# Key sums beside the second product transposed and added in one VectorE operation; their reciprocals stored and spread from GpSimd's queue

## The chip, the cores and the metric

The kernel runs on one core of a Trainium2 chip. Its time is the device time of one execution in microseconds (us). The profile calls the engines PE (TensorE, matmuls), PEld (TensorE's weight loads), DVE (VectorE), ACT (ScalarE), POOL (GpSimd) and SP (SyncE, which here only issues DMAs). Each of them works through its own instructions in the order in which the program gives them.

## The reference

Attention with normalised queries and keys, and after it two matrix products with a squared ReLU between them. All tensors are float32; q, k and v have 8 batches of 12 heads, 448 rows and 64 columns, and the products have 3584 rows, 768 columns and 2048 hidden columns.

```python
q_n, k_n = rmsnorm(q, g_q), rmsnorm(k, g_k)
scores = scale * np.matmul(q_n, k_n.transpose(0, 1, 3, 2))
scores = scores - np.max(scores, axis=-1, keepdims=True)
attn = np.exp(scores)
attn = attn / (np.sum(attn, axis=-1, keepdims=True) + 1e-09)
attn_out = np.matmul(attn, v)
...
x = attn_out.transpose(0, 2, 1, 3).reshape(B * S, H * D)
h = x @ w_in
r = np.maximum(h, 0.0)
return (r * r) @ w_out
```

## The kernel before

**Stages.** The batches are taken two at a time, in four spans. A span has two batches of six head pairs, so 12 pairs, which I call units, numbered through (`i`). The attention of the first span runs alone. After it each span has a first product (line 1040) and a second product (line 1087). Both are written as seven block products in place of eight (a Strassen form), so that VectorE and GpSimd have sums of blocks to make beside them. In the first three spans the second product and the attention of the next span are woven together: one is a generator with a step for each matmul, the other a generator with five steps for each unit, and the loop at the end of the kernel takes from both in turn. In the first span this stage also holds `combine` (lines 1001 to 1005), the block sums for its second product, on VectorE. Only in these three stages does the changed code run, 12 units in each, 36 in all.

**A unit of attention there** (function `attention`, line 945). Keys lie on partitions. `scores(i, c)` multiplies a chunk of 128 keys (`c` from 0 to 2; chunk 3 has the last 64) with all queries, into one of two PSUM buffers, and ScalarE writes the exponential (line 761) into one of five places: four tiles `pr` and the half `qkT[:, 1]`, taken in turn, `places[(3 * i + c) % 5]`; chunk 3 has a tile of its own, `half`. `values(i)` (line 837) multiplies the exponentials with v, one unit later. For the denominators VectorE adds the four chunks into `acc` (`add_up`, lines 782 and 784), 128 partitions by 896 columns, and `fold(i)` adds over the partitions: a transpose in blocks of 32 by 32 (line 792), a sum over 32 (line 793), three small copies that bring the four quarters of the partitions side by side (line 795), a sum (797), a reciprocal (798) and a small transpose (799) into `square`. The transpose of line 792 needs a scratch tile; it takes the place that `scores(i + 1, 0)` writes next.

**The factors' way.** At the end of unit `i` SP stores `square` to a small tensor in DRAM (line 990, `factors`, one of two in turn, 28 rows of 128 bytes). In the next unit, behind `values`, ScalarE's queue issues two DMAs (`spread`, line 805) that read each head's 1,792 bytes back and write them to 64 partitions of `xT` each. `finish(i)` then adds the two halves of the value product (line 873) and multiplies them with these factors in place (line 875); that product is the input of the next first product.

**What stands around it in each queue**, by the order of the program in a unit `i`:

- SP: the input loads of unit i+3 (line 668), at its start; the loads of v (685, 687); between them the weight blocks for the second product (`sw`, line 649) and its output stores (line 1078); the store of line 990 last. All DMAs of a queue are issued in this order, and one that must wait holds those behind it.
- ScalarE: the exponentials of chunks 0 and 1; the spread of unit i-1; the exponentials of chunks 3 and 2; the copy of half a value product out of PSUM (line 966); the scaling of transposed queries (736); squares (711). Copies out of PSUM for the second product (line 1096) fall in between.
- GpSimd: a power (line 724, `norm_by_squares`) and two products (726) that normalise unit i+2; in the second batch of a span, block sums of `xT` (`combine_x`, lines 885 to 890), except for the last pair, whose sums are on VectorE.
- VectorE: the adds into `acc`, the sums for the norms (718 to 723), the transposes of queries and keys (735), lines 873 and 875, `fold`, and what the second product asks of it (1075 and 1098 to 1106).

In the last unit of a stage there are no scores any more: `values`, line 805 and `finish` of the 12th unit follow each other directly.

Of the kernel before, what the change touches and what calls it, by code (L numbers as in the profile page):

```python
# [12 lines left out]
ALU = mybir.AluOpType  # L13
AX = mybir.AxisListType.X
# [372 lines left out]
def attention_then_ffn_bounded(  # L387
# [35 lines left out]
    nc = tc.nc  # L423

    B, H, S, D = q.shape
# [12 lines left out]
    NF = S // P  # L438
# [27 lines left out]
    xT = consts.tile([P, 2, NPAIR, S], F32, name="xT")  # L466
# [188 lines left out]
    places, halves, rests = [], [], {}  # L655
    sums = {"out": [dram.tile([2 * S // 32, 32], F32, name=f"factors{n}") for n in range(2)]}

    def load(i):
        if i < NAT:
            load_q(nc, qk, q, i)  # L660
            load_k(nc, qk, k, i)
            return

        b, h0 = i // NPAIR, 2 * (i % NPAIR)
        for s, src in enumerate((q, k)):
            dst = by_squares(i, 0)[:, s]
            for n in range(4):
                nc.sync.dma_start(dst[n * 32:(n + 1) * 32],
                                  src[b, h0 + n // 2, :, n % 2 * 32:n % 2 * 32 + 32]
                                  .rearrange("(g t) e -> t g e", t=32))  # L670
# [38 lines left out]
    def squares(i):  # L709
        raw, qkn = (by_squares(i, n).rearrange("p s g e -> p (s g e)") for n in range(2))  # L710
        nc.scalar.activation(qkn, raw, AF.Square)

    def norm_by_squares(i):
        raw, qkn = (by_squares(i, n) for n in range(2))
        NG = S // 32
        half = small.tile([P, 2 * NG], F32, tag="half", name="half")
        other = small.tile([P, 2 * NG], F32, tag="other", name="other")
        nc.vector.tensor_reduce(half, qkn.rearrange("p s g e -> p (s g) e"), AX, ALU.add)
        for n in range(4):
            m = n ^ 1  # L720
            nc.vector.tensor_copy(other[n * 32:(n + 1) * 32], half[m * 32:(m + 1) * 32])
        nc.vector.tensor_tensor(half, half, other, ALU.add)
        nc.vector.tensor_scalar(half, half, 1.0 / D, 1e-6, ALU.mult, ALU.add)  # L723
        nc.gpsimd.tensor_tensor(half, half, mhalf, ALU.pow)  # L724
        for s in range(2):
            nc.gpsimd.tensor_tensor(  # L726
                qkn[:, s], raw[:, s],
                half[:, s * NG:(s + 1) * NG].rearrange("p g -> p g ()").to_broadcast([P, NG, 32]), ALU.mult)
        normed[i] = qkn

    def transposes(i):

        qkn = normed.pop(i)
        for s in range(2):
            nc.vector.transpose(qkT[:, 0, s], qkn[:, s].rearrange("p g e -> p (g e)"))
        nc.scalar.activation(qkT[:, 0, 0], qkT[:, 0, 0], AF.Copy, scale=gains[:, 0:1])
# [11 lines left out]
    def scores(i, c):  # L748


        if i >= NAT:
            sc = ps_s.tile([P, 2, 512], F32, tag="s", name="sc")
            n = S if c < NF else S // 2
            for h in range(2):
                rows = slice(h * D, (h + 1) * D)
                for m, part in enumerate(sides):
                    keys = slice(c * P + m * D, c * P + (m + 1) * D) if c < NF else slice(NF * P, S)
                    of = slice(0, S) if c < NF else slice(m * n, (m + 1) * n)
                    nc.tensor.matmul(sc[part, h, 0:n], qkT[rows, 0, 1, keys], qkT[rows, 0, 0, of], start=True, stop=True)  # L759
            pr = probs[i, c] = places[(NF * i + c) % len(places)] if c < NF else halves[i % 2]  # L760
            nc.scalar.activation(pr, sc[:, :, 0:n], AF.Exp)  # L761
            return
        at = i % 2
        sc = ps_s.tile([SP, 2, 512], F32, tag="s", name="sc")
        for h in range(2):
            rows = slice(h * D, (h + 1) * D)
            nc.tensor.matmul(sc[:, h, 0:S], qkT[rows, at, 1, c * SP:(c + 1) * SP], qkT[rows, at, 0, :],
                             start=True, stop=True)
        pr = probs[i, c] = places[(NJ * i + c) % len(places)][:SP]
        for h in range(2):  # L770
            nc.scalar.activation(pr[:, h], sc[:, h, 0:S], AF.Exp, scale=rstds[i][:, 1, 2 * c + h:2 * c + h + 1])
# [4 lines left out]
    def add_up(i, c):  # L776

        acc = acc_of(i)
        if i >= NAT and c == NF:
            for m, rows in enumerate(sides):  # L780
                part = acc[rows, :, m * S // 2:(m + 1) * S // 2]
                nc.vector.tensor_tensor(part, part, probs[i, c][rows], ALU.add)  # L782
            return
        nc.vector.tensor_tensor(acc, probs[i, 0] if c == 1 else acc, probs[i, c], ALU.add)  # L784

    def fold(i):


        NG = S // 32
        acc, quarters = sums["acc"].rearrange("p h q -> p (h q)"), sums["quarters"]  # L790
        turned = places[NF * (i + 1) % len(places)].rearrange("p h q -> p (h q)")
        nc.vector.transpose(turned, acc)  # L792
        nc.vector.tensor_reduce(quarters[:, 0], turned.rearrange("p (n k) -> p n k", k=32), AX, ALU.add)  # L793
        for n in range(1, 4):
            nc.vector.tensor_copy(quarters[0:32, n], quarters[n * 32:(n + 1) * 32, 0])
        square, turned = sums["square"][:, 0], sums["square"][:, 1]
        nc.vector.tensor_reduce(square[:, 0:2 * NG], quarters[0:32].rearrange("p a n -> p n a"), AX, ALU.add)
        nc.vector.reciprocal(square[:, 0:2 * NG], square[:, 0:2 * NG])
        nc.vector.transpose(turned, square)

    def spread(i):

        b, hp = divmod(i, NPAIR)
        for h in range(2):
            nc.scalar.dma_start(xT[h * D:(h + 1) * D, b % 2, hp],
                                sums["out"][i % 2].rearrange("(h g) t -> h () (g t)", h=2)[h].to_broadcast([D, S]))

    def sums_for(work):
# [10 lines left out]
    def values(i, chunks=range(NJ)):  # L819
        if 0 in chunks:  # L820
            pavs[i] = ps_o.tile([P, S], F32, tag="o", name="pav") if i >= NAT or i % 2 == 0 else bank("pav", 1)
        if i >= NAT:
            return later_values(i)
        for c in chunks:
            for h in range(2):
                nc.tensor.matmul(pavs[i][h * D:(h + 1) * D, :], vs[i][:SP, h, c, :], probs[i, c][:, h, :],
                                 start=(c == 0), stop=(c == NJ - 1))
# [117 lines left out]
    def attention(first):  # L945


        last = first + 2 * NPAIR
        for i in range(first, last + 1):
            if i < last:  # L950
                scores(i, 0)
                scores(i, 1)
            if i + 3 < min(last + 2, B * NPAIR):
                load(i + 3)
            if i == first:
                yield
            if i > first:
                values(i - 1)
                spread(i - 1)
            if i < last:  # L960
                add_up(i, 1)
                scores(i, 3)
                scores(i, 2)
            if i > first:
                rest = halves[(i - 1) % 2].rearrange("p h q -> p (h q)")
                nc.scalar.copy(rest, rests[i - 1])
                rests[i - 1] = rest
            if i + 2 < last:
                norm_by_squares(i + 2)
            yield  # L970
            if i + 1 < last:
                transposes(i + 1)
            if i < min(last, B * NPAIR - 1):
                load_v(i + 1)
            yield
            if i < last:
                add_up(i, 2)
                add_up(i, 3)
            if i > first:
                finish(i - 1)  # L980
            if i + 3 < last:
                squares(i + 3)
            yield
            if i < last:
                fold(i)
            if i > first:
                combine_x(i - 1)
            yield
            if i < last:
                nc.sync.dma_start(sums["out"][i % 2], sums["square"][0:2 * S // 32, 1])  # L990
            yield


# [277 lines left out]
```

## Time and profile before

| | us |
|---|---|
| three runs | 1384.28, 1383.55, 1379.16; median 1383.55 |
| the profiled execution, whole | 1382.71 |
| its span in the trace | 1380.9 |
| attention alone, first product of span 0 | 0 to 133, 133 to 265 |
| second product with attention beside it, three times | 265 to 471, 599 to 795, 923 to 1120 |
| first products of spans 1 to 3 | 471 to 599, 795 to 923, 1120 to 1247 |
| last second product | 1247 to 1381 |

The stages' limits are read from the timeline of TensorE, to about a microsecond. The granted clock of TensorE was 0.998 of full speed in the profiled execution. The lines of `fold` and of the factors' way, from the profile's answers on single source lines (duration of one in ns as least, median and most; first and last start in us):

```profile
L792 DVE STREAM_TRANSPOSE pr<-acc x28: 1065/1104/1111, 294.6 to 1085.4; 128x896 f32<-128x896 f32 x28
L792 DVE STREAM_TRANSPOSE qkT<-acc x8: 1064/1102/1105, 277.4 to 1099.7; 128x896 f32<-128x896 f32 x8
L793 DVE TENSOR_REDUCE quarters<-pr x28: 1085/1086/1089, 295.7 to 1086.5; 128x28 f32<-128x896 f32 x28
L793 DVE TENSOR_REDUCE quarters<-qkT x8: 1086/1086/1087, 278.6 to 1100.9; 128x28 f32<-128x896 f32 x8
...
L990 SPq DMA_DIRECT2D factors<-square x36: 324/353/605, 281.3 to 1104.2; - x36
L805 ACTq DMA_DIRECT2D xT<-factors x72: 452/553/1006, 282.7 to 1106.0; - x72
```

In a line of the timeline the numbers are the start and the length in us, then come engine, line, operation and tiles (out<-in); in brackets stands the engine's idle time ahead of it and what ended it. A row of DMA issues gives the issuing queue, the count, the size of one and the median time from issue to landing.

### The profile page before, as it was taken

To read this page: it belongs to the slowest core of one execution; us is meant where nothing else is said; L and a number is where in the kernel's file an instruction comes from. 1 tells how busy PE (TensorE), PEld (TensorE's weight loads), DVE (VectorE), ACT (ScalarE), POOL (GpSimd) and SP (SyncE) were. 2 spreads that over 40 slices of the span, in tenths; PEclk is the share of its full clock that TensorE was granted. 3 is DMA by queue.
4 is the path that set the end of the run, shared out by engine and by line. 5 is a ranking of instruction groups with operands and counts; after the bars stand their busy time and mean duration, and the time that the engine had idled before them with its cause. 6 is when DMAs were issued, how large, how long until landed. Compare 5 with 4: busy or idle time off the path is not lost.

```text
span 1380.9 us, 16875 instructions
## 1 busy us (share of the span) xinstructions
PE 1345.1 (97%) x5602; PEld 635.8 (46%) x5602; DVE 844.3 (61%) x1470; ACT 425.2 (31%) x657; POOL 576.4 (42%) x397
## 2 busy tenths in 40 slices
PE   8989999998999999999999999999999999999997
PEld 3333455443444455444444455444444445554553
DVE  6989676499987433567987623458888723332111
ACT  7876565432332011233333111233333211110000
POOL 6998887543443122635444122445445212220000
PEclk9999999999999999999999999999999999999999
DMA  9687998654566333345666433345565343334443
GB/s 247 189 232 195 314 392 299 182 112 93 124 143 139 94 86 91 100 109 113 140 136 132 103 103 87 99 107 117 121 139 114 96 104 91 86 90 104 104 114 67
DMA packets 436685, 190.13 MB, mean 138 GB/s; under 512 B 283244, under 2 KB 434540, under 8 KB 436588
## 3 DMA queue, kind: packets, MB, share of 16 engines
q1 hardware_dynamic: 426988, 180.23, 50.9%
q10 hardware_dynamic: 9472, 8.72, 2.4%
q8 instruction: 47, 0.77, 0.2%
q14 instruction: 50, 0.41, 0.1%
q0 software_dynamic: 128, 0.00, 0.0%
HBM read 155.72 MB, written 33.16 MB: 137 GB/s over the span
## 4 chain that ended last, share of the span: by engine, by line
PE 71%; DVE 11%; DMA 6%; POOL 5%; issue 3%; ACT 2%; SPq 1%; ACTq 1%; DVEq 0%; POOLq 0%
PE ps L1087 25%; PE pd L1040 10%; PE pa L1040 10%; PE pc L1040 10%; PE pb L1040 5%; PE sc L759 4%; PE pav L837 3%; DMA factors<-square 2%; DMA xT<-factors 2%; POOL rstd L702 2%; DVE quarters L793 1%; DVE acc L782 1%; DVE acc L784 1%; POOL gC L566 1%; DVE pr L792 1%
## 5 line engine op out<-in xcount | busy, mean ns | idle before, releaser
L1087 PE MATMUL ps<-gT,sw 128*128 128x448 f32 x768 | 299.5, 543 | 5.0 <-DVE p L1106 4.2
L724 POOL TENSOR_TENSOR half<-half,mhalf 128x28 f32<-128x28 f32 x36 | 173.7, 4824 | 258.9 <-DVE half L723 207.1
L1087 PE MATMUL ps<-gC,sw 128*128 128x448 f32 x576 | 225.5, 543 | 4.3 <-ACT p L1096 2.6
L1017 POOL TENSOR_TENSOR gT<-gT 128x448 f32<-128x448 f32 x96 | 93.6, 976 | 303.7 <-ACT gT L1013 303.7
L1087 PEld LDWEIGHTS ps<-gT,sw 128*128 128x128 f32 x768 | 143.6, 190 | 156.0 <-issue 146.1
L1087 PEld LDWEIGHTS ps<-gC,sw 128*128 128x128 f32 x576 | 107.7, 190 | 118.4 <-issue 110.1
L1040 PE MATMUL pa<-xT,sw 128*128 128x448 f32 x384 | 154.9, 539 | 0.0
L1013 ACT ACTIVATE gT<-gT 128x448 f32<-128x448 f32 x96 | 55.4, 577 | 311.8 <-DVE gT L1055 311.8
L761 ACT ACTIVATE pr<-sc 128x896 f32<-128x896 f32 x87 | 77.2, 914 | 123.6 <-PE sc L759 50.2
L759 PE MATMUL sc<-qkT 64*64 64x448 f32 (+1 forms) x1152 | 111.6, 498 | 3.3 <-ACT pr L761 3.0
L1040 PEld LDWEIGHTS pa<-xT,sw 128*128 128x128 f32 x384 | 72.9, 190 | 71.7 <-issue 70.4
L1055 DVE TENSOR_TENSOR gT<-z,pd 128x448 f32<-128x448 f32 x32 | 19.9, 620 | 99.8 <-PE pd L1040 99.7
L1040 PE MATMUL pb<-xC,sw 128*128 128x448 f32 x192 | 77.5, 539 | 1.5 <-issue 1.5
L1040 PE MATMUL pc<-xC,sw 128*128 128x448 f32 x192 | 77.5, 540 | 0.8 <-DMA sw<-w1s 0.8
L1040 PE MATMUL pd<-xT,sw 128*128 128x448 f32 x192 | 77.8, 541 | 0.0
L726 POOL TENSOR_TENSOR qk<-qk,half 128x448 f32<-128x448 f32 x72 | 76.5, 1083 | 2.8
L1040 PE MATMUL pd<-xC,sw 128*128 128x448 f32 x192 | 77.5, 539 | 0.0
L1040 PE MATMUL pc<-xT,sw 128*128 128x448 f32 x192 | 77.4, 539 | 0.0
L837 PE MATMUL pav<-pr,vt 64*64 64x448 f32 x348 | 72.8, 537 | 2.6 <-DVE half L873 2.6
L572 POOL TENSOR_TENSOR gC<-gC 128x384 f32<-128x384 f32 x64 | 73.8, 1173 | 2.5
L837 PE MATMUL rest<-pr,vt 64*64 64x448 f32 x348 | 72.8, 537 | 0.0
L1047 DVE TENSOR_TENSOR z<-p,pb 128x448 f32<-128x448 f32 x32 | 19.8, 619 | 81.1 <-PE pb L1040 81.1
(136 smaller groups left out, 1874.6 us busy)
## 6 DMA issues: line engine op xcount, KB each, us to landing
sw<-w1s SPq DMA_DIRECT2D x224, 192.0 KB, 2.4
sw<-w2s SPq DMA_DIRECT2D x168, 256.0 KB, 3.4
w1s<-gC SPq DMA_DIRECT2D x8, 1344.0 KB, 7.7
w2s<-gC SPq DMA_DIRECT2D x8, 1344.0 KB, 8.4
out_dram<-osb SPq DMA_DIRECT2D x184, 56.0 KB, 2.0
qk<-in_q_dram SPq DMA_DIRECT2D x144, 56.0 KB, 2.9
qk<-in_k_dram SPq DMA_DIRECT2D x144, 56.0 KB, 2.6
xT<-factors ACTq DMA_DIRECT2D x72, 112.0 KB, 3.5
```

The costliest lines, as they stand in the source:

```text
L572: nc.gpsimd.tensor_tensor(*[blocks_of(n)[:, i] for i in (dst, x, y)], op)
L702: nc.gpsimd.tensor_tensor(flat, flat, mhalf[:SP, 0:4 * NJ], ALU.pow)
L724: nc.gpsimd.tensor_tensor(half, half, mhalf, ALU.pow)
L726: nc.gpsimd.tensor_tensor(qkn[:, s], raw[:, s], half[:, s * NG:(s + 1) * NG].rearrange("p g -> p g ()").to_broadcast([P, NG, 32]), ALU.mult)
L759: nc.tensor.matmul(sc[part, h, 0:n], qkT[rows, 0, 1, keys], qkT[rows, 0, 0, of], start=True, stop=True)
L761: nc.scalar.activation(pr, sc[:, :, 0:n], AF.Exp)
L837: nc.tensor.matmul(into, vs[i][rows, h, c, :], probs[i, c][rows, h, :], start=(c == 0), stop=(c == NF), skip_group_check=True)
L1013: nc.scalar.activation(g, src, AF.Relu)
L1017: nc.gpsimd.tensor_tensor(g, g, g, ALU.mult)
L1040: nc.tensor.matmul(ps, stream[n + i][:, c], rhs[:, c], start=first and c == 0, stop=c == HC - 1, skip_group_check=not first)
L1055: add(g, x, ps, ALU.add)
L1087: nc.tensor.matmul(ps, stream[n][:, c % 4], rhs_of[i][:, c], start=c == 0, stop=c == HF - 1)
```

## The change

`fold` loses its scratch: the transpose of line 792 and the sum of line 793 become one `tensor_reduce` with `apply_transpose`, which reads `acc` and writes `quarters`. The store of `square` moves from SP's queue to GpSimd's. The spread moves from ScalarE's queue to GpSimd's, and from the next unit, behind `values`, to the end of its own unit, directly behind the store.

```diff
         NG = S // 32
         acc, quarters = sums["acc"].rearrange("p h q -> p (h q)"), sums["quarters"]
-        turned = places[NF * (i + 1) % len(places)].rearrange("p h q -> p (h q)")
-        nc.vector.transpose(turned, acc)
-        nc.vector.tensor_reduce(quarters[:, 0], turned.rearrange("p (n k) -> p n k", k=32), AX, ALU.add)
+        nc.vector.tensor_reduce(quarters[:, 0], acc.rearrange("p (n k) -> p n k", k=32), AX, ALU.add,
+                                apply_transpose=True)
         for n in range(1, 4):
...
         for h in range(2):
-            nc.scalar.dma_start(xT[h * D:(h + 1) * D, b % 2, hp],
+            nc.gpsimd.dma_start(xT[h * D:(h + 1) * D, b % 2, hp],
                                 sums["out"][i % 2].rearrange("(h g) t -> h () (g t)", h=2)[h].to_broadcast([D, S]))
...
             if i > first:
                 values(i - 1)
-                spread(i - 1)
             if i < last:
...
             if i < last:
-                nc.sync.dma_start(sums["out"][i % 2], sums["square"][0:2 * S // 32, 1])
+                nc.gpsimd.dma_start(sums["out"][i % 2], sums["square"][0:2 * S // 32, 1])
+                spread(i)
             yield
```

## The prediction

> **What bounds the kernel now.** I read the busy line first, then the span cut into its stages, then every idle stretch of TensorE in the stages that the change touches, and last what stood ahead of the releaser of each.
>
> ```profile
> PE 1345.1 (97%) x5602; PEld 635.8 (46%) x5602; DVE 844.3 (61%) x1470; ACT 425.2 (31%) x657; POOL 576.4 (42%) x397
> ...
> 265.00:471.00 206.00, 196.19 (x1099) 88.89 (x1092) 172.38 (x326) 60.34 (x85) 80.86 (x39) 1.00 0.55 117
> 471.00:599.00 128.00, 128.00 (x350) 64.11 (x352) 48.79 (x86) 25.09 (x44) 43.25 (x37) 1.00 0.36 97
> 599.00:795.00 196.00, 194.42 (x1101) 90.15 (x1094) 155.69 (x298) 59.62 (x84) 80.69 (x41) 1.00 0.56 123
> 923.00:1120.00 197.00, 193.84 (x1093) 90.05 (x1090) 155.63 (x298) 59.48 (x83) 80.31 (x41) 1.00 0.52 116
> ```
>
> In a window's row the second number is the length, the third TensorE's busy time, the fifth VectorE's. TensorE is the bound: a first product (471 to 599) leaves it no gap. Only three windows hold the change (second product with attention beside it); they leave TensorE 9.8, 1.6 and 3.2 us, 14.6 us together. That is the most this change can win. The first of them, with VectorE at 172.4 of 206 us, has two thirds of it. TensorE's gaps in the timeline, with their releasers:
>
> ```profile
> 312.36 0.59 PE L837 MATMUL pav<-pr,vt 64*64 64x448 f32 x1 [1.78 <-DVE half L873]
> 316.17 0.61 PE L759 MATMUL sc<-qkT 64*64 64x224 f32 x8 [0.95 <-ACT pr L761]
> 326.61 3.25 PE L1087 MATMUL ps<-gC,sw 128*128 128x448 f32 x8 [1.70 <-POOL qk L726]
> 348.29 0.59 PE L837 MATMUL pav<-pr,vt 64*64 64x448 f32 x1 [0.86 <-DVE half L873]
> ...
> 465.31 6.28 PE L1087 MATMUL ps<-gT,sw 128*128 128x448 f32 x16 [2.42 <-DVE p L1106]
> ...
> 655.67 3.27 PE L1087 MATMUL ps<-gC,sw 128*128 128x448 f32 x8 [1.16 <-ACT p L1096]
> ...
> 979.42 3.27 PE L1087 MATMUL ps<-gC,sw 128*128 128x448 f32 x8 [1.46 <-ACT p L1096]
> ```
>
> Grouped, all gaps of the three windows are: (a) 2.64 us for L873 (VectorE late); (b) 3.2 us, nine times 0.15 to 0.95, for an exponential; (c) 4.32 us before three `ps` matmuls (1.70, 1.16, 1.46); (d) 4.24 us in the last unit of each stage (2.42, and likewise 0.26 and 1.56). The 1.70 is put down to POOL, but what frees a bank there is the copy L1096, as in the other two. The stretch before it:
>
> ```profile
> 316.45 0.20 DVE L799 STREAM_TRANSPOSE square<-square 32x32 f32<-32x32 f32 x1
> ...
> 319.96 0.60 SPq L990 DMA_DIRECT2D factors<-square  x1
> ...
> 323.14 1.11 ACTq L805 DMA_DIRECT2D xT<-factors  x2
> 324.30 0.54 ACT L761 ACTIVATE half<-sc 128x448 f32<-128x448 f32 x1 [7.38 <-PE ps L1087]
> ...
> 325.95 0.56 ACT L1096 COPY p<-ps 128x448 f32<-128x448 f32 x1
> ```
>
> The square is ready at 316.65, but SP issues its store 3.3 us later, behind output stores; ACT's spread waits for that store, and two exponentials and two copies wait behind the spread. And (b):
>
> ```profile
> ACT pr L761 <- DVE quarters L793: 44.8, 8, 7.9
> ACT pr L761 <- DVE quarters L795: 19.7, 3, 6.7
> ```
>
> With the `qkT` place (14.1 and 5.2) ACT waits 83.8 us for `fold`, since the exponential of the next unit overwrites the scratch that L793 still reads.
>
> [...] The trace shows both halves alone (1.104 and 1.086 us), not together. [...] the three copies of L795 take 0.57 us mostly, but 1.24 us at 776.48, beside a POOL subtraction.
>
> **The change part by part.**
>
> *1. One operation for L792 and L793.* 36 instructions of 1.104 us go, 39.7 us of VectorE, 13.2 us per window. For the fused one: low bound 1.09 us (it reads the 896 elements that L793 reads), high bound 2.19 us (the two now). I take 1.1. The first window's VectorE then has 159 us, near the 155.7 of the other two, where no gap of kind (a) exists: minus 2.64 us. If the operation costs 2.19, this gain is nil.
>
> *2. The scratch goes.* The next unit's exponential then needs only its own scores: its place was last read by the value matmuls of the previous unit and by that unit's adds, over half a unit before. What is late next is the score matmul itself. Gap (b) goes: minus 3.2 us; ACT's 83.8 us are mostly idle and worth nothing more.
>
> *3. Store off SP, spread off ACT.* SP loses 36 issues of 0.35 us and 87.1 us of waiting for L799, so input loads behind it go earlier. ACT loses 72 issues of 0.55 us and the wait for the store: gap (c) goes, minus 4.32 us.
>
> *4. What POOL takes on.* Per unit one store and two spreads, and between them the wait for the store. Its nearest rows are the four loads of `gains`:
>
> ```profile
> L358 POOL DMA_DIRECT2D gains<-in_g_q_dram x2: 532/628/723, 1.2 to 2.0; - x2
> ...
> gains<-in_g_q_dram POOLq DMA_DIRECT2D x2, 0.2 KB, 2.7
> ```
>
> 64 rows each, as each half of a spread has, but 4 bytes a row instead of 1,792. Issue: 0.55 to 0.72 us; I take 0.6. Landing of the store: 1.3 us as SP shows in 778.69 to 780.05, 2.7 us as `gains` shows; I take 2.5. So POOL is held 0.05 + 2.5 + 2 x 0.6 = 3.75 us after L799, with bounds 2.5 and 4.3. Queued behind is the power L724 of unit i+3 (4.8 us), then its products L726 (2.2). L724 now starts 3.8 to 6.5 us after L799 (316.65 to 320.47; 298.39 to 304.07; 663.45 to 667.93), for it waits for VectorE's L723, and that stays. So the delay is 0 to 0.6 us. Who waits for L726: the transposes L735, 10 us later (311.16 to 322.50), and SP's load L668 into the same place, 6 to 10 us later. The cover is the 14.65 us unit (`ps` starts at 680.15, 694.79 and 709.44 in the chain of waits) against POOL's 7.1 us of work; if it were gone, each us of POOL is a us of the unit.
>
> *5. The last unit.* Here the product L875 has no cover. From L799's end to L875 it takes 6.05, 6.43 and 5.96 us now: store 1.3, issue, landing 3.5 (2.8 to 4.8). On POOL: 0.05 + 2.5 + 0.6 to the second issue, then 3.5 to 4: 6.7 to 7.2, less the 1.1 us by which `fold` ends earlier. Between -0.5 and +1.5 us in each stage; I take +0.2, +0.6 in all. Gap (d) stays.
>
> Sum: 2.64 + 3.2 + 4.32 = 10.2 us won, 0.6 lost in part 5, and 1.1 us that I leave for new small gaps (before the change the quieter windows had 0.15 us of kind (b), but POOL's and VectorE's overlaps shift): net -8.5 us. The profiled execution took 1382.71 us with a span of 1380.9, so 1.8 us lie around it: 1372.4 + 1.8 = 1374.2. It was 0.84 us under the median shown, 1383.55; so 1375.0.
>
> **The rivals.**
> - *A, forecast:* as above, 1375.
> - *B, the fused operation costs as much as the two.* For: nothing shows the two together. [...] Then 2.64 is kept, and the last unit has no earlier `fold`, +1.1 in three stages: -8.5 + 2.6 + 3.3 = -2.6, 1381.
> - *C, the gaps move.* VectorE in the first window stays at 80% (159 of 199 us) with bursts, [...] the last units lose 1.5 us each. For: 2.65 us at 308.99 for two adds that take 1.27 elsewhere, beside POOL's L726. About half of 10.2 remains less 1.5: -4, 1379.5.
> - *D, slower: POOL becomes the bound.* Place: its queue between L799 and the next L724. [...] With 7.1 us of work (8.2 in three units with a subtraction) in 14.65, the chain may take 7.5 us (6.4). If a spread issue took 3 us: 2.5 + 6 = 8.5, over by 1.0 in seven units and 2.1 in three, 13.3 us a stage, 40 in three, plus some 7 in the last units, less 10: 1420. It decides from an issue of about 2.5 us, four times what `gains` shows; that is the case against.
>
> **How the numbers follow.** A 0.58, B 0.12, C 0.20, D 0.10. About 0.5%, 6.9 us, is what a measurement of this kernel can tell from no change: faster means under 1376.6. A's own range is 1371 to 1379 (half of part 5's bounds, and the residue from 0 to 3), two thirds to three quarters of it under that limit: 0.42 faster, 0.16 same. B gives 0.02 and 0.10, C 0.07 and 0.11, with 0.02 slower. D is slower. Together 0.51, 0.37, 0.12. The range goes from 1369.5, where nearly all of the 14.6 us are gone, to 1385, which takes in B, C and the scatter of the three runs; D is left out.
>
> **What would show it.** Right: a VectorE row of about 1.1 us x36 in place of L792 and L793; no ACT wait for `quarters`; no gap before `ps` with an ACT copy as releaser; windows of about 199, 195 and 196 us. Wrong: a fused row near 2.2 us; POOL issues of `xT` over 2 us, or L735 waiting for L726; last-unit gaps over 3 us.

## The result, and the profile after

The changed kernel takes 1370.26 us (median of 6 runs, 1367.65 to 1373.89), the kernel before 1381.36 (6 runs): a ratio of 0.9922, 95% interval 0.9904 to 0.9941, so 0.8% faster, about 11 us. Run twice more, beside the experiments, it gave 0.9903 (0.9883 to 0.9923) and 0.9911 (0.9892 to 0.9930). The profiled execution took 1369.76 us with a span of 1367.8, against 1382.71 and 1380.9.

The busy line of the page and TensorE's gaps in its timeline, after (the columns are those of before; the lines from 791 on have moved up by one or two, so L872 and L874 are the old L873 and L875, and L1095 and L1105 the old L1096 and L1106):

```profile
PE 1341.9 (98%) x5602; PEld 638.1 (47%) x5602; DVE 811.9 (59%) x1434; ACT 426.8 (31%) x657; POOL 633.2 (46%) x505
```

```profile
309.36 0.59 PE L836 MATMUL pav<-pr,vt 64*64 64x448 f32 x1 [1.51 <-DVE half L872]
...
454.51 6.28 PE L1086 MATMUL ps<-gT,sw 128*128 128x448 f32 x16 [2.02 <-DVE p L1105]
...
1099.00 7.97 PE L1086 MATMUL ps<-gT,sw 128*128 128x448 f32 x16 [1.96 <-DVE p L1105]
```

These three are all the gaps that the three changed stages still have, 5.5 us where there were 14.4. Gone are all nine before an exponential, all three behind ScalarE's copy, one of the two for the old L873 and one of the three in the last units. What stands in the place of the two old operations, of the store and of the spread (answers on single lines):

```profile
L791 DVE TRANSPOSE_TENSOR_REDUCE quarters<-acc x36: 1062/1104/1112, 275.5 to 1084.5; 128x28 f32<-128x896 f32 x36
```

```profile
L988 POOL DMA_DIRECT2D factors<-square x36: 525/598/625, 278.5 to 1089.0; - x36
...
DMA to landing us min/median/max: 1.6/2.7/4.2
```

```profile
L804 POOL DMA_DIRECT2D xT<-factors x72: 516/530/556, 281.8 to 1091.7; - x72
...
DMA to landing us min/median/max: 2.6/3.4/6.0
```

The fused operation lasts 1.104 us, as long as the transpose alone did. A spread's issue takes 0.53 us on GpSimd with rows of 1,792 bytes; the four-byte rows of `gains` took 0.53 to 0.72, and ScalarE's issue of the same spread 0.55 before. Only the store's issue is longer from GpSimd, 0.60 us against 0.35 from SP, and it lands later, after 2.7 us in the median against the 1.3 that the prediction read from SP.

**Where the time came from.** The length of a stage is a better measure than its listed gaps. I take it from the first `ps` of a second product to the first `pa` after it. For the first stage of the changed kernel, from TensorE's timeline:

```profile
263.86 1.77 PE L1086 MATMUL ps<-gT,sw 128*128 128x448 f32 x4
...
460.63 2.42 PE L1039 MATMUL pa<-xT,sw 128*128 128x448 f32 x6
```

That is 196.77 us. The same stretch before, 205.66 us:

```profile
265.77 1.77 PE L1087 MATMUL ps<-gT,sw 128*128 128x448 f32 x4
...
471.43 2.42 PE L1040 MATMUL pa<-xT,sw 128*128 128x448 f32 x6
```

Ten stages in seven of the 14 profiles have no listed gap and take 192.74 us each, so this serves as the floor. Two further stages without a listed gap, both of a kernel with more work on VectorE, take up to 0.4 us more.

| kernel, one execution each | stage 1 | stage 2 | stage 3 | over the floor, sum |
|---|---|---|---|---|
| before | 205.66 | 195.09 | 196.66 | 19.2 |
| changed | 196.77 | 192.74 | 196.66 | 8.0 |
| changed, second profile | 196.23 | 192.74 | 193.52 | 4.3 |
| changed, third profile | 196.22 | 192.74 | 193.32 | 4.1 |

The stages give 11.2, 14.9 and 15.1 us. Before the change there is one profile only, so these differences share its scatter. The first profile's third stage stands no shorter than before, because 1.7 us of it are a spell at half clock (last section). The first profile's whole span gained 13.1: the other 1.9 us lie ahead of the first stage, where the change does nothing; that stage begins between 263.1 and 269.1 us in all executions but one (the kernel with a loaded GpSimd), whatever the kernel. In the three profiles of the changed kernel the start differs by up to 5.2 us and the sum over the floor by up to 3.9, and what is left of the span is the same, 1095.8 to 1096.0 us. So these two account for how far the three differ; the runs without a profile could not be taken apart like this.

### The profile page after: what moved, and what is told of

The parts are those of the page before. It is cut to its first block, busy times and chain, and to the rows that moved or that the text cites. A ratio compares the mean times of both kernels' runs of the same rounds, so it can differ in the third digit from the quotient of the medians.

```text
span 1367.8 us, 16894 instructions
## 1 busy us (share of the span) xinstructions
PE 1341.9 (98%) x5602; PEld 638.1 (47%) x5602; DVE 811.9 (59%) x1434; ACT 426.8 (31%) x657; POOL 633.2 (46%) x505
## 4 chain that ended last, share of the span: by engine, by line
PE 86%; POOL 6%; DVE 4%; DMA 2%; issue 2%; ACT 1%; DVEq 0%; POOLq 0%; ACTq 0%
PE ps L1086 35%; PE pa L1039 10%; PE pd L1039 10%; PE pc L1039 10%; PE sc L759 7%; PE pav L836 6%; PE pb L1039 5%; POOL rstd L702 2%; POOL gC L566 1%; POOL gC L572 1%; DMA xT<-factors 1%; POOL qk L704 1%; DMA sw<-w1s 1%; ACT gT L771 0%; PE tot L850 0%
## 5 line engine op out<-in xcount | busy, mean ns | idle before, releaser
L804 POOL DMA_DIRECT2D xT<-factors x72 | 38.0, 532 | 90.1 <-DMA factors<-square 61.0
L726 POOL TENSOR_TENSOR qk<-qk,half 128x448 f32<-128x448 f32 x72 | 75.0, 1061 | 2.8
```

The costliest lines, as they stand in the source:

```text
L726: nc.gpsimd.tensor_tensor(qkn[:, s], raw[:, s], half[:, s * NG:(s + 1) * NG].rearrange("p g -> p g ()").to_broadcast([P, NG, 32]), ALU.mult)
L804: nc.gpsimd.dma_start(xT[h * D:(h + 1) * D, b % 2, hp], sums["out"][i % 2].rearrange("(h g) t -> h () (g t)", h=2)[h].to_broadcast([D, S]))
```

## The experiments

Theory: the gaps are of separate kinds with separate causes (VectorE late, the scratch, the DMA wait in ScalarE's queue, the last unit), so that parts of the change win separately and add up. Its rivals: one part does it all; GpSimd is close to being the bound; a removed wait only moves.

**The two parts alone.** The fused operation alone takes `fold`'s hunk of the change and leaves both DMAs where they were; the queues alone take the other hunks and leave `fold`.

> The kernel before with the fused operation alone; store and spread stay on SP and ScalarE. Theory (the gaps add up by their kinds): the gaps before pav for L873 (2.6 us) and those before sc for an exponential (3.2 us) go, those before ps behind ScalarE's copy (4.3 us) stay, so about 6 us below before, some 5 us above the changed kernel. Rival (ScalarE's and SP's queues held everything, VectorE was only late because of them): within 2 us of before.

> The changed queues alone; fold keeps its transpose, its sum and the scratch in the next unit's place. Theory: only the gaps before ps behind ScalarE's copy go (4.3 us), and the last units have no earlier fold, up to 1 us more each: 2 to 4 us below before, 7 to 9 us above the changed kernel. Rival: within 2 us of the changed kernel.

Measured: 1371.83 us, 0.9947 of before (0.9932 to 0.9962), and 1374.95 us, 0.9960 (0.9949 to 0.9972). Each won somewhat more than expected, 7 and 5.5 us, and neither rival held. On another chip they were run again beside the whole change.

> The changed kernel, beside its two parts alone on one chip. Theory (gaps of different kinds, which add up): 9 to 13 us below before, about the sum of what the two parts win alone, less what both of them win (the last units' earlier product). Rival (one part does all of it): within 2 us of the better part.

> The fused operation alone, queues as before. Theory: 6 to 8 us below before, 2 to 5 us above the changed kernel of this call; the gap before ps behind ScalarE's copy is there in two or three stages.

> The queues alone, fold as before. Theory: 4 to 6 us below before, 4 to 8 us above the changed kernel of this call; no gap behind ScalarE's copy, gaps for L873 and for exponentials in the first stage.

| one chip, 26 runs of before | median us | ratio | 95% interval | stages over the floor |
|---|---|---|---|---|
| changed | 1369.83 | 0.9911 | 0.9892 to 0.9930 | 4.1 |
| fused alone | 1371.83 | 0.9936 | 0.9920 to 0.9953 | 7.2 |
| queues alone | 1377.03 | 0.9970 | 0.9957 to 0.9983 | 12.2 |

In shares of 1382 us the parts win 8.8 and 4.1 us, and the whole 12.3: they add up within what can be told. On this chip alone the fused part is only 2.0 us behind the whole, and the intervals overlap; what tells them apart is that its ratios, 0.9947 and 0.9936, both lie above the three of the whole change, 0.9903 to 0.9922, by some 4 us in the mean. So no one part does it all, and the fused part wins about two thirds. None of the three profiles has a half-clock spell in its stages. TensorE's gaps in the fused kernel, without one of 0.22 us for L872 and one of 0.97 in a last unit:

```profile
308.56 0.59 PE L836 MATMUL pav<-pr,vt 64*64 64x448 f32 x1 [1.47 <-DVE half L872]
...
321.69 3.25 PE L1086 MATMUL ps<-gC,sw 128*128 128x448 f32 x8 [2.17 <-POOL qk L726]
...
644.24 3.27 PE L1086 MATMUL ps<-gC,sw 128*128 128x448 f32 x8 [0.73 <-ACT p L1095]
```

No gap waits for an exponential, and two of the three behind ScalarE's copy are there (2.17 and 0.73; in the kernel's first profile 2.27 and 1.18). With the queues alone it is the other way round; all gaps of its first stage but that of the last unit:

```profile
297.31 0.98 PE L759 MATMUL sc<-qkT 64*64 64x448 f32 x8 [0.20 <-ACT pr L761]
311.07 0.59 PE L837 MATMUL pav<-pr,vt 64*64 64x448 f32 x1 [1.90 <-DVE half L873]
314.88 0.61 PE L759 MATMUL sc<-qkT 64*64 64x224 f32 x8 [0.95 <-ACT pr L761]
315.69 0.98 PE L759 MATMUL sc<-qkT 64*64 64x448 f32 x8 [0.20 <-ACT pr L761]
347.34 0.61 PE L759 MATMUL sc<-qkT 64*64 64x224 f32 x8 [0.95 <-ACT pr L761]
348.15 0.98 PE L759 MATMUL sc<-qkT 64*64 64x448 f32 x8 [0.20 <-ACT pr L761]
363.54 0.98 PE L759 MATMUL sc<-qkT 64*64 64x448 f32 x8 [0.20 <-ACT pr L761]
```

Six gaps for an exponential, 2.70 us, and none behind the copy. So the exponentials' gaps go with `fold` and the copy's with the queues. The parting is not clean, though: the copy's gap of the third stage is gone with the fused operation alone too, and the second gap for the old L873 with the queues alone too, in both profiles of each. That is why the parts, counted over the stages, win 12.0 and 7.0 us, more together than the 15.1 of the whole.

**VectorE's time without the scratch.** The fused operation is issued twice onto one output:

```diff
         nc.vector.tensor_reduce(quarters[:, 0], acc.rearrange("p (n k) -> p n k", k=32), AX, ALU.add,
                                 apply_transpose=True)
+        nc.vector.tensor_reduce(quarters[:, 0], acc.rearrange("p (n k) -> p n k", k=32), AX, ALU.add,
+                                apply_transpose=True)
```

> The changed kernel with the fused operation issued twice onto the same output: VectorE's work is as before, but there is no scratch. Theory: the gaps before sc and those behind ScalarE's copy are gone, those for L873 come back (about 2.6 us) and the last units are 1.1 us later: 3 to 6 us above the changed kernel, nearly all in the first of the three stages and the last units. Rival (VectorE's work is hidden, the scratch was what counted): within 1.5 us of the changed kernel.

Measured: 1372.32 us, 0.9952 (0.9937 to 0.9967), and stages of 200.15, 192.76 and 193.15 us. The first stage is 3.9 us above those of the changed kernel's second and third profiles, the other two differ by 0.4 at most. Of the 3.9 us, 1.7 are a spell at half clock right behind this stage's longest pause (last section). That pause, for the old L873, is 2.74 us instead of 1.5 to 1.6, and two gaps for an exponential, 0.47 and 0.20, are there. So VectorE's 1.1 us a unit counts in the first stage only, the one that also holds `combine`, and mostly through this one pause; and since VectorE works as long as before here, it is the missing scratch that leaves only two gaps for an exponential, where the queues alone had six, and four in their first profile. The last units did not show the expected lateness. The second fused operation lasted 1.111 us.

**The spread back on ScalarE, the store on GpSimd.**

```diff
-            nc.gpsimd.dma_start(xT[h * D:(h + 1) * D, b % 2, hp],
+            nc.scalar.dma_start(xT[h * D:(h + 1) * D, b % 2, hp],
...
                 values(i - 1)
+                spread(i - 1)
...
-                spread(i)
```

> The changed kernel with the spread back on ScalarE in its old place, behind values; the store stays on GpSimd. Theory: the store no longer waits behind SP's output stores, so ScalarE waits little for it, and most of the gaps behind ScalarE's copy stay away: 0 to 3 us above the changed kernel. Rival (any DMA wait in ScalarE's queue costs): 4 us or more above, with the ps gaps back.

Measured: 1371.00 us, 0.9942 (0.9927 to 0.9957), beside the fused kernel's 1371.83 and 0.9947 on the same chip; no gap behind the copy in its profile, stages of 194.49, 194.85 and 194.82 us. So, as far as one profile shows it, what held ScalarE's copies up was the store's late issue on SP (3.3 us after the small transpose in the unit that the prediction shows), and with the store on time the spread may stay where it was. Two gaps of the last units (1.84 and 1.81) and one of 1.52 for L872 are what it has left over the floor. The run times don't show what the store's move is worth here: they don't tell this kernel from the fused one, and the changed kernel was not run beside them.

**The store back on SP, the spread on GpSimd.**

```diff
-                nc.gpsimd.dma_start(sums["out"][i % 2], sums["square"][0:2 * S // 32, 1])
+                nc.sync.dma_start(sums["out"][i % 2], sums["square"][0:2 * S // 32, 1])
```

> The changed kernel with the store back on SP; the spread stays on GpSimd. Theory: the store again waits behind SP's output stores in some units, so GpSimd's spread and the power behind it come up to 3 us later there, which the slack before the transposes hides; the last units' store lands sooner: within 2 us of the changed kernel. Rival (GpSimd's queue may not wait any longer than it does): 3 us or more above it.

Measured: 1368.28 us, 0.9908 (0.9889 to 0.9927), beside 0.9911 for the changed kernel on the same chip: no difference. GpSimd's waits there, and then in the changed kernel's first profile:

```profile
POOL xT L804 <- DMA factors<-square: 99.2, 21, 10.1
```

```profile
POOL half L724 <- DVE half L723: 72.1, 30, 10.0
POOL factors L988 <- DVE square L798: 71.1, 34, 5.2
POOL xT L804 <- DMA factors<-square: 61.0, 23, 4.2
```

The numbers are us in total, times, and the longest. GpSimd waits up to 10.1 us for one store. In this profile the first stage has 2.82 us of gaps for L872 (0.73 and 2.09), more than the changed kernel's 1.6, and the last units have none; the stages together are 0.8 us shorter than in the third profile of the changed kernel, so the longer waits were within GpSimd's slack. In the profiles either move cures the gap behind ScalarE's copy; making both is not needed for that. In run time only the kernel with the spread moved is shown to be level with the changed one.

**GpSimd loaded.** One more power of 28 columns in each norm, its result not read:

```diff
+        nc.gpsimd.tensor_tensor(other, half, mhalf, ALU.pow)
         nc.gpsimd.tensor_tensor(half, half, mhalf, ALU.pow)
```

> The changed kernel with a second power of the same size on GpSimd in each norm (4.8 us, its result is not read). GpSimd then has 7.1 + 4.8 us of work and is held some 3.7 us by store and spread, 15.6 us in a unit of 14.65. Theory: GpSimd's free time in the changed kernel is about 4 us a unit, so it becomes the bound by about 1 us in each of nine or ten units of three stages, and its slack of some 10 us before the transposes is used up only late in a stage: 5 to 25 us above the changed kernel. Rival (GpSimd has room to spare): within 2 us of the changed kernel.

Measured: 1417.70 us, 1.0275 of before (1.0251 to 1.0300), 51 us above the changed kernel on that chip: twice the most expected. A unit of GpSimd in its second stage, from the timeline, and then the same stretch of the changed kernel:

```profile
668.43 4.83 POOL L724 TENSOR_TENSOR other<-half,mhalf 128x28 f32<-128x28 f32 x1
673.35 4.79 POOL L725 TENSOR_TENSOR half<-half,mhalf 128x28 f32<-128x28 f32 x1
678.22 1.84 POOL L727 TENSOR_TENSOR qk<-qk,half 128x448 f32<-128x448 f32 x2
680.00 0.60 POOL L989 DMA_DIRECT2D factors<-square  x1
682.86 1.06 POOL L805 DMA_DIRECT2D xT<-factors  x2 [2.26 <-DMA factors<-square]
683.93 5.00 POOL L724 TENSOR_TENSOR other<-half,mhalf 128x28 f32<-128x28 f32 x1
```

```profile
668.33 4.82 POOL L724 TENSOR_TENSOR half<-half,mhalf 128x28 f32<-128x28 f32 x1 [0.38 <-DVE half L723]
673.24 1.84 POOL L726 TENSOR_TENSOR qk<-qk,half 128x448 f32<-128x448 f32 x2
677.07 0.60 POOL L988 DMA_DIRECT2D factors<-square  x1 [1.99 <-DVE square L798]
679.27 1.05 POOL L804 DMA_DIRECT2D xT<-factors  x2 [1.60 <-DMA factors<-square]
682.96 4.83 POOL L724 TENSOR_TENSOR half<-half,mhalf 128x28 f32<-128x28 f32 x1 [2.64 <-DVE half L723]
```

Loaded, GpSimd runs from one unit into the next with no wait but that for the store, 15.5 us a round; in this stretch every wait for VectorE is gone. In the changed kernel's unit it waits twice for VectorE, 1.99 and 2.64 us, 4.6 us together (3.2 a unit over the three stages); that is the slack left beside the moved DMAs, and 4.8 us of load exceed it. The stages are 17.8, 13.9 and 11.5 us longer than in the second profile of the changed kernel, more than a round's excess explains. The last spread then comes late too: the last units' gaps are 7.49, 7.10 and 4.56 us. And behind TensorE's pauses come spells at half clock (last section), which cost 9.8 us of matmul time in the three stages. Another 4 us come ahead of the first stage, where this profile has a pause of 5.05 us at 146.23. The same load with the DMAs in their old queues was not run; by an estimate from the prediction's 7.1 us of GpSimd work, 4.8 more would fit into a unit of 14.65.

**The last units.** Two ways to shorten their gap. In the first, store and spread of the last unit are issued from ScalarE's queue; in the second, TensorE's generator is taken two steps further ahead of `finish` in the last unit, which puts the adds L1103 and L1105 in front of L872 and L874 on VectorE:

```diff
-                nc.gpsimd.dma_start(sums["out"][i % 2], sums["square"][0:2 * S // 32, 1])
-                spread(i)
+                queue = nc.gpsimd if i + 1 < last else nc.scalar
+                queue.dma_start(sums["out"][i % 2], sums["square"][0:2 * S // 32, 1])
+                spread(i, queue)
```

```diff
-                    while done < min(total, total * (u + 1) // (10 * NPAIR + 1)):
+                    while done < min(total + 2 * (u > 10 * NPAIR), total * (u + 1) // (10 * NPAIR + 1)):
```

> The changed kernel once more, so that the others of this call have it on the same chip, and to see what of its gaps recurs. Theory: 0.990 to 0.994 of before. The gaps of the last units (2.02, 0 and 1.96 us in the first profile) come from how long two DMAs took to land, so they differ by up to 2 us from one execution to the next; rival: they belong to the stage and come back as 2, 0, 2.

> The changed kernel, but in the last unit of each stage store and spread are issued from ScalarE's queue. Theory: the way from the small transpose to the product L874 is then about 6 us as before the change, in place of 6.6 us or more on GpSimd's queue, so the last units' gaps shrink by 0.5 to 1 us each, 1 to 2 us in all: hardly more than can be measured. Rival (the queue costs nothing there): no shorter way, the same gaps.

> The changed kernel with one thing moved: in the last unit of a stage the two VectorE adds that free a ps bank come ahead of the pair that waits for the spread. Theory: the wait for the spread stays on VectorE, but TensorE no longer waits for it: no ps gap in the last units and no low clock behind one, some 4 to 6 us below the changed kernel, all in the ends of the three stages. Rival: the wait moves to the next bank or to the first product, and the stages take as long as before.

| one chip, 11 runs of before | median us | ratio | 95% interval | stages |
|---|---|---|---|---|
| changed | 1366.69 | 0.9903 | 0.9883 to 0.9923 | 196.23, 192.74, 193.52 |
| last unit on ScalarE | 1366.01 | 0.9899 | 0.9880 to 0.9918 | 194.49, 192.74, 192.74 |
| adds first | 1367.74 | 0.9912 | 0.9892 to 0.9933 | 194.48, 192.74, 192.74 |

Both do what was meant: no `ps` gap is left in a last unit, and the stages lose 2.5 us against this chip's changed kernel. The way from the small transpose to L874, on ScalarE's queue:

```profile
1089.07 0.20 DVE L798 STREAM_TRANSPOSE square<-square 32x32 f32<-32x32 f32 x1
1089.31 0.34 ACTq L989 DMA_DIRECT2D factors<-square  x1
1090.61 1.11 ACTq L804 DMA_DIRECT2D xT<-factors  x2
...
1094.06 0.62 DVE L874 TENSOR_TENSOR xT<-half,xT 128x448 f32<-128x448 f32 x1 [0.83 <-DMA xT<-factors]
```

That is 4.8 us, where the same way took 6.6 in the changed kernel's first profile (1088.74 to 1095.33). But no run time tells either from the changed kernel: the medians lie 0.7 us below and 1.0 us above it. The expected 4 to 6 us of the second assumed gaps, and a low clock behind them, as in the first profile; in the second the last units had 1.42, 0 and 0.51 us. They do differ from one execution to the next, as the theory had it. No version is shown to beat the changed kernel.

## Why the prediction was right

The forecast was 1375.0 for a median of 1383.55, that is 8.5 us less; by the ratios 10.8, 13.4 and 12.3 us were won. Direction, place and the main mechanisms were right. The size was too small, by 2.3 to 4.9 us. The measured median, 1370.26, lies below rival A's own range (1371 to 1379) and 0.8 us above the low end of the whole range, which the repeats on other chips reach and pass (1369.83 and 1366.69); that it fell inside is in part luck. By terms of the sum:

- *The fused operation at 1.1 us* (part 1): measured 1.104. The 1.1 was the author's estimate, taken at its low bound, L793's 1.09 us; no trace ahead of the change showed the operation. Rival B is out.
- *Gap (a), 2.64 us, goes* (part 1): half wrong. The second of its two gaps went, but with the queues alone too, so the fused operation was not its only cure. The first, 1.78 before, stayed at 1.51, 1.58 and 1.63 in three profiles. The step that failed was to compare VectorE's load over the whole stage with that of the other two. In this unit the two halves of L782 take 2.69 us, right beside POOL's L726, and L872 starts directly behind them, at 308.68:

```profile
305.94 2.22 POOL L726 TENSOR_TENSOR qk<-qk,half 128x448 f32<-128x448 f32 x2
305.95 2.69 DVE L782 TENSOR_TENSOR acc<-acc,half 64x448 f32<-64x448 f32 x2
```

  The queue's order there was not changed. That the overlap sets the length of this gap fits the kernel with the store on SP, where only one of the two halves lay beside L726 (0.62 and 1.25 us) and the gap was 0.73; no experiment moved the two apart. It is also what rival C pointed to, the two adds that are slow beside L726.
- *Gap (b), 3.2 us, goes* (part 2): right; none is left in the changed kernel, 2.70 us are left with the queues alone. The exponentials' waits for `quarters` are gone from ScalarE's list, and those of `pr` wait for their score matmul:

```profile
ACT pr L761 <- PE sc L759: 121.5, 54, 7.4
```

- *Gap (c), 4.32 us, goes* (part 3): right. In the profiles the late store alone or the spread's place alone is enough to cure it.
- *GpSimd held 3.75 us after the small transpose* (part 4): from 312.51 to 316.06, 3.55 us; the store landed after 2.7 us in the median, where 2.5 were taken. The power still waits for L723, 30 times. That GpSimd can become the bound, as rival D has it, the loaded kernel shows (51 us above the changed one); but D's price, the issue of a spread, is 0.53 us and not 2.5.
- *The last units lose 0.2 us each* (part 5): they had 4.24 us of gaps, then 3.98, 1.93 and 1.67 in the three profiles. So they gained 0.3 to 2.6 us instead of losing 0.6, and in four of nine stages more than the 0.5 us of the lower bound (2.42 to 1.42 and 1.36, 1.56 to 0.51 and 0.31). The earlier `fold` outweighed the slower way through GpSimd: with the fused operation alone the last units had 0.55 and 0.97 us in the two profiles, with the queues alone 3.28 and 4.43.
- *The reserve of 1.1 us for new small gaps:* there are none in the three profiles.
- *The sum of the gaps itself*, 14.4 us, taken for the stages' loss, with 14.6 us as "the most this change can win": too small. The stages stood 19.2 us over the floor, and two profiles won 14.9 and 15.1. A gap in the listing begins at the modelled end of the matmul ahead, 0.54 us after its start, though without a gap the next one starts 0.376 us after it; that hides 0.16 us of each gap. Measured, a stage with one or two gaps and no half-clock spell is mostly longer than the floor by its gaps and 0.23 to 0.27 us more for each (three third stages by 0.45 to 0.66). For 17 gaps at 0.25 us that is 4.3 us, nearly all of the difference of 4.8; the change removed 14 of them, 3.5 us.

With 3.5 us from the hidden parts, 1.1 from the reserve, 0.9 to 3.2 from the last units and 1.5 lost at (a), the forecast of 8.5 becomes 12.5 to 14.8. The second and third profiles gave 14.9 and 15.1 in their stages, the first 11.2 and, without its half-clock spell, 12.9.

## What to carry to other kernels

A DMA that waits for another DMA belongs in a queue whose next work has slack, and the store ahead of it in a queue where nothing stands in front: here either half of that removed the gaps behind ScalarE's copy (4.32 us before), and the first alone was level with the whole change. Before such a move, add up the time that the receiving engine waits for others in each unit: it was 4.6 us in the unit shown, and a load of 4.8 us cost 51 us. A scratch borrowed from the next consumer's place is a wait that stands in no engine's busy time (here 83.8 us of ScalarE's); and where a bound stage has a floor that recurs from run to run (here 192.74 us), compare stages with it, not sums of listed gaps, and look at the clock in each stage first: one spell at half clock was 1.7 us.

## What the runs showed of the hardware that was not expected

After the last gap of the changed kernel's first profile the sixteen `ps` matmuls took 7.97 us instead of 6.28. The trace grants TensorE half its clock from 1099.41 to 1102.82, and there the matmuls start 0.75 us apart instead of 0.376. This spell costs 1.7 us, so the pause cost 3.9 us in all; the whole of stage 3's gain went into it.

A pause of 2.42 us before the change, and one of 2.02 in stage 1 of this same profile, left the clock at 1.00. What told them apart can be read from the traces. In the 14 profiles every spell ahead of TensorE's last matmul lasts 3.41 us or a multiple of it, and within one profile their starts lie whole multiples of 3.413 us apart (21.51, 96.60 and 315.06 in the kernel with two fused operations: 22 and 64 of them). So in these profiles the clock changed on a grid of windows of 3.413 us. Here are the windows around four pauses (length, then what TensorE, its weight loads, VectorE, ScalarE and GpSimd are busy, then the granted clock): two of the changed kernel,

```profile
450.88:454.29 3.41, 1.61 (x5) 0.52 (x3) 3.27 (x6) 0.00 (x0) 0.00 (x0) 1.00 0.01 2
454.29:457.70 3.41, 3.19 (x9) 1.70 (x10) 1.99 (x4) 0.00 (x0) 0.00 (x0) 1.00 0.35 60
1096.00:1099.41 3.41, 1.45 (x4) 0.49 (x3) 3.31 (x6) 0.00 (x0) 0.00 (x0) 1.00 0.01 2
1099.41:1102.82 3.41, 3.41 (x6) 1.64 (x5) 1.35 (x3) 0.00 (x0) 0.00 (x0) 0.50 0.45 74
```

the 2.42 us before the change, and the 2.74 us of the kernel with two fused operations:

```profile
460.57:463.98 3.41, 2.33 (x7) 0.86 (x5) 2.19 (x4) 0.00 (x0) 0.00 (x0) 1.00 0.01 3
463.98:467.39 3.41, 2.08 (x6) 1.15 (x7) 3.10 (x6) 0.00 (x0) 0.00 (x0) 1.00 0.13 23
```

```profile
311.64:315.06 3.42, 1.13 (x12) 0.51 (x16) 3.32 (x5) 0.65 (x1) 1.10 (x1) 1.00 0.02 5
315.06:318.47 3.41, 3.41 (x28) 1.57 (x24) 3.18 (x9) 0.00 (x0) 0.00 (x0) 0.50 0.00 0
```

The idle time within one window tells these four apart. With 1.80 us idle (3.41 less 1.61) the next window kept the full clock, with 1.96 and 2.29 it had half of it. The 2.42 us lie across a limit, 1.08 in one window and 1.33 in the next, and cost nothing more. In all 14 profiles together, each of the 24 windows at full clock in which TensorE idles for 1.85 us or more is followed by one at half clock; of the full-clock windows with 1.80 us or less, none is. So the luck of where a pause lay on the grid decided over 1.7 us. The start of the first stage goes with the same spells: with none ahead of it, it begins at 263.1 to 264.5 us, with one at 265.8 to 268.0, with two at 267.0 to 269.1 (all kernels but the loaded one).

Beside GpSimd's block sums VectorE's small copies took longer: three of `quarters` took 2.15 us beside L888 and L889 in the kernel with the adds first (at 1082.95), and 0.55 us at 311.02 in the changed kernel, where GpSimd waited.
